# Computing part of an attention output projection transposed: 512 + 128 output columns per block instead of 320 + 320

## The chip, the cores and the metric

The kernel runs on one core of one Trainium2 chip. The metric is the device time of one execution in microseconds (us). Most executions of one kernel agree within 0.1 to 0.2%, so differences of a few tenths of a microsecond can only be read in the trace, and differences of about one need the median of several executions.

## The reference, cut to what matters

```python
x = A_x                                   # 1 x 2048 x 640, bf16
xn = _layernorm(x)
s = attention(xn) @ wo                    # 32 heads of 192; the last 512 keys of each cache; wo: 6144 x 640
g = silu(ffn(xn))                         # SwiGLU FFN, 640 -> 1536 -> 640
return x + s * g
```

The kernel handles the heads in 16 pairs, and the 2048 rows in 4 blocks of 512. For each pair and block it computes queries, scores, the product with V (PV), and adds the pair's share of `@ wo` to a sum in SBUF, the core's working memory.

## The kernel before

Every matmul of the main loop contracts 64 of the 128 partitions. `lo` is partitions 0 to 63 and `hi` is 64 to 127, and the two halves of TensorE's rows ("row groups" below) work side by side, each on a bank of its own of PSUM, the memory that matmuls write to. The output projection of one tile of 128 rows is one unit in two parts; between the parts the two row groups swap banks, which a small GpSimd memset with semaphores makes safe:

```python
    def wo_turn(st, i, qt, turn):
        ps = st["sc"]
        for j in range(3):                       # 3 chunks of 128 of the pair's 384 head columns
            for k, r in enumerate((lo, hi)):     # low, high, low, high, ...
                n = k ^ turn
                m = nc.tensor.matmul(
                    ps[:, n, 0:HD], OTs[i][r, 3 * qt + j, :], pairs[i // NB]["wo"][r, j, n * HD : (n + 1) * HD],
                    start=(turn == 0 and j == 0), stop=(turn == 1 and j == 2), skip_group_check=True,
                )
                after(m, st)
        if turn == 0:
            turned(m, st)
```

`OTs[i]` is the attention output of a block, normalised by ScalarE (`O_b`) and turned by a DMA transpose (`OT_b`), in two halves of two row tiles each. `HD` is 320. The projection of a block is issued two blocks later, woven between the PV halves of that block:

```python
    def woven(i):
        (a, b), (w, x, y, z) = (pv(i, 0), pv(i, 1)), (wo_tile(i - 2, qt) for qt in range(4))
        for part in (*a[:2], drop, w[0], *b[:2], w[1], x[0], *a[2:], x[1], y[0], *b[2:], y[1], z[0]):
            part()
        held.append(z[1])
```

In the stretch of a pair the loads of a coming pair stand behind blocks 0, 1 and 2, all on SyncE's queue:

```python
            if b == 0 and pr + 2 < NPAIR:
                load_k(pr + 2)
            elif b == 1 and pr + 2 < NPAIR:
                load_wq(pr + 2)
            elif b == 2:
                load_wo(pr + 1)
```

The softmax here doesn't subtract the row's maximum and nothing guards it: scores larger than these inputs give would overflow.

## Time and profile before

| | before |
|---|---|
| median of the first 3 runs | 922.86 us (922.59 to 923.6) |
| profiled run | 922.45 us, of which the page shows a span of 920.7 us |
| matmuls in the trace | 11086 |
| TensorE, VectorE, ScalarE busy | 99%, 63%, 52% |

The prediction below shows the head of the page, the waits and the windows. Here are the groups of the page that the change touches: line, engine, operation, output and inputs, shape, count, then busy us and mean ns of one, and idle time of the engine before them.

```profile
L440 PE MATMUL mm<-xnT,wq_p 64*128 64x512 bf16 x1890 | 240.2, 376 | 0.0
L601 DVE TENSOR_TENSOR sacc<-sacc,sc 128x640 f32<-128x640 f32 x200 | 164.2, 821 | 87.0 <-PE sc L576 87.0
L576 PE MATMUL sc<-wo_p,OT_b 64*128 64x320 bf16 x2592 | 217.3, 296 | 0.0
L479 PE MATMUL mm<-V_p,p_t 64*128 64x193 bf16 x3520 | 186.4, 242 | 0.0
```

L440 is the queries, L576 the output projection, L479 PV, L601 the add of a row tile to its sum. A matmul's record (376 ns at 512 columns) is longer than the distance to the next start on its row group (216 ns), so the records overlap and no busy share tells whether TensorE is full. The starts do.

For comparing traces I split the span into a **ledger**: opening (up to the first down-projection matmul), FFN (from there to the first 64-row query matmul), each pair (first score to the next pair's first score, called the **period** below), the last pair (first score to the last matmul) and the tail (start of the last matmul to the end). Before: 38.21, 128.88, then 41.67, 45.96, twelve times 47.03 and 47.26, last pair 49.23, tail 4.00 (the 1.09 us from the first query to the first score makes up the rest).

### The profile page before, as it was taken

Reading aid. Unit: us, or ns where it says so; the run is one execution under the profiler, and the core shown is the slowest. Engines: PE = TensorE matmul, PEld = TensorE weight load, DVE = VectorE, ACT = ScalarE, POOL = GpSimd, SP = SyncE. Lnnn points to the kernel's source line nnn. Section 1 sums busy time; section 2 is a strip of 40 time slices with the busy share of each in tenths; the row PEclk is TensorE's granted clock in tenths of the full one; section 3 lists DMA queues with packets and bytes.
Section 4 is the critical chain, followed back from the end, with each engine's and each line's share of the span. In section 5 each row is a group of like instructions: output and inputs, shape, how many; then the busy total and the mean of one; then the engine's idle time right before and its main releaser. Section 6 shows DMA issues by size and latency. Waiting matters only on the chain.

```text
span 920.7 us, 25767 instructions
## 1 busy us (share of the span) xinstructions
PE 914.6 (99%) x11086; PEld 625.9 (68%) x11102; DVE 575.8 (63%) x847; ACT 474.6 (52%) x850; POOL 101.9 (11%) x390
## 2 busy tenths in 40 slices
PE   9999999999999999999999999999999999999998
PEld 5455556575858585868686767676777777676666
DVE  6343331467676767676766667676767676767656
ACT  4222222556464646565556565655555555556461
POOL 0000000000000000000000000000000000002978
PEclk9999999999999999999999999999999999999999
DMA  9330510045644444435536262635271717163524
GB/s 308 64 75 18 110 35 1 1 78 89 92 74 85 82 83 83 79 87 70 97 62 104 60 108 53 113 48 119 44 122 36 130 37 126 31 129 86 130 62 142
DMA packets 243762, 77.18 MB, mean 84 GB/s; under 512 B 224576, under 2 KB 243648, under 8 KB 243648
## 3 DMA queue, kind: packets, MB, share of 16 engines
q1 hardware_dynamic: 243216, 75.14, 41.9%
q8 instruction: 87, 1.43, 0.7%
q10 hardware_dynamic: 432, 0.39, 0.2%
q14 instruction: 27, 0.22, 0.1%
HBM read 39.45 MB, written 2.62 MB: 46 GB/s over the span
## 4 chain that ended last, share of the span: by engine, by line
PE 98%; POOL 0%; DMA 0%; DVE 0%; issue 0%; POOLq 0%; ACT 0%; DVEq 0%
PE mm L440 22%; PE sc L576 19%; PE sc L454 18%; PE mm L479 16%; PE sc L277 11%; PE mm L299 6%; PE sc L548 2%; PE mm L531 2%; POOL ob L636 0%; PE gu L277 0%; PE mm L548 0%; PE mm L312 0%; DMA x_t<-in_A_x_dram 0%; PE sc L479 0%; PE sc L531 0%
## 5 line engine op out<-in xcount | busy, mean ns | idle before, releaser
L458 ACT ACTIVATE p_t<-sc 128x1024 bf16<-128x1024 f32 x254 | 253.0, 1023 | 128.2 <-PE sc L454 128.2
L445 DVE TENSOR_REDUCE qT<-mm 128x512 bf16<-128x1024 f32 x189 | 231.1, 1223 | 95.3 <-PE mm L440 92.8
L509 ACT ACTIVATE O_b<-mm,r 128x192 bf16<-128x192 f32 x486 | 165.0, 422 | 180.8 <-issue 156.3
L440 PE MATMUL mm<-xnT,wq_p 64*128 64x512 bf16 x1890 | 240.2, 376 | 0.0
L601 DVE TENSOR_TENSOR sacc<-sacc,sc 128x640 f32<-128x640 f32 x200 | 164.2, 821 | 87.0 <-PE sc L576 87.0
L576 PE MATMUL sc<-wo_p,OT_b 64*128 64x320 bf16 x2592 | 217.3, 296 | 0.0
L454 PE MATMUL sc<-qT,khat 64*128 64x512 bf16 x1524 | 198.2, 376 | 0.0
L479 PE MATMUL mm<-V_p,p_t 64*128 64x193 bf16 x3520 | 186.4, 242 | 0.0
L479 PEld LDWEIGHTS <-p_t 64*128 64x128 bf16 x3584 | 162.9, 93 | 12.1
L440 PEld LDWEIGHTS <-wq_p 64*128 64x128 bf16 x1890 | 105.7, 94 | 93.4 <-issue 0.5
L576 PEld LDWEIGHTS <-OT_b 64*128 64x128 bf16 x2592 | 140.4, 94 | 21.4
L454 PEld LDWEIGHTS <-khat 64*128 64x128 bf16 x1536 | 85.9, 94 | 79.8
L564 POOL MEMSET turn_t<- 128x1 f32 x328 | 32.5, 99 | 691.9 <-PE mm L479 469.7
L285 DVE TENSOR_TENSOR hT<-sc,sg 128x512 bf16<-128x512 f32 x46 | 31.7, 691 | 83.7 <-ACT sg L284 83.7
L284 ACT ACTIVATE sg<-sc 128x512 bf16<-128x512 f32 x46 | 27.3, 597 | 73.4 <-PE sc L277 71.9
L277 PE MATMUL sc<-xnT,wg_sb 128*128 128x512 bf16 (+1 forms) x248 | 59.5, 353 | 0.7
L277 PE MATMUL sc<-xnT,wu_sb 128*128 128x512 bf16 (+1 forms) x259 | 60.2, 354 | 0.1
L299 PE MATMUL mm<-wd_sb,hT 128*128 128x320 bf16 x384 | 56.6, 299 | 0.0
L498 DVE RECIPROCAL r<-mm 128x4 f32<-128x4 f32 x124 | 22.6, 182 | 46.9 <-PE mm L479 36.1
L299 PEld LDWEIGHTS <-hT 128*128 128x128 bf16 x384 | 37.6, 98 | 18.9
L277 PEld LDWEIGHTS <-wu_sb 128*128 128x128 bf16 x285 | 27.1, 98 | 26.9 <-issue 0.2
L277 PEld LDWEIGHTS <-wg_sb 128*128 128x128 bf16 x285 | 27.1, 98 | 22.7
(69 smaller groups left out, 374.9 us busy)
## 6 DMA issues: line engine op xcount, KB each, us to landing
wo_p<-in_A_wo_dram SPq DMA_DIRECT2D x16, 480.0 KB, 4.4
K_p<-in_A_k_cache_dram SPq DMA_DIRECT2D x32, 192.0 KB, 3.3
V_p<-in_A_v_cache_dram SPq DMA_DIRECT2D x32, 192.0 KB, 3.0
wq_p<-in_A_wq_dram SPq DMA_DIRECT2D x64, 80.0 KB, 3.0
wq_p<-in_A_wq_dram SPq DMA_DIRECT2D x16, 160.0 KB, 3.4
x_r<-in_A_x_dram SPq DMA_DIRECT2D x16, 160.0 KB, 4.7
x_t<-in_A_x_dram SPq DMA_DIRECT2D x14, 160.0 KB, 3.0
OT_b<-O_b SPq DMA_TRANSPOSE x124, 3.0
```

The lines of the kernel that those rows point to most:

```text
L277: nc.tensor.matmul(out, w_sb[:, c, f * P : (f + 1) * P], xnT[:, c, qc], start=(c == 0), stop=(c == NC - 1),)
L285: nc.vector.tensor_tensor(hTs[b][:, f, :], u, sg[:], ALU.mult)
L299: nc.tensor.matmul(dn[:, 0:HD], hTs[b][:, f, ti * P : (ti + 1) * P], wd_sb[:, f, cols], start=(f == 0), stop=(f == NF - 1),)
L440: nc.tensor.matmul(q_ps[:, h, :], pairs[pr]["wq"][r, c, j * P : (j + 1) * P], xnT[r, c, b * 512 : (b + 1) * 512], start=(c == 0), stop=(c ...
L445: nc.vector.reduce_sum(qTs[i][:, j, :], q_ps[:, :, :].rearrange("p h n -> p n h"), axis=AX.X)
L454: nc.tensor.matmul(sc[:, h, :], khat[r, j, ks], qT[r, j, :], start=(j == 0), stop=(j == 2))
L458: nc.scalar.activation(p_t[:, :, :], sc[:, :, :], ACT.Exp, scale=scale)
L479: m = nc.tensor.matmul(acc[:, k, h * 256 : h * 256 + Dh + 1], Ps[i][kc][r, h, qt * P : (qt + 1) * P], V_p[r, kc, h, 0 : Dh + 1], start=(p ...
L509: nc.scalar.activation(O_b[:, qt, h, :], a_k[:, h, 0:Dh], ACT.Copy, scale=r[:, k, h, :])
L564: st["turn"] = nc.gpsimd.memset(turn_t[:], 0.0)
L576: m = nc.tensor.matmul(ps[:, n, 0:HD], OTs[i][r, 3 * qt + j, :], pairs[i // NB]["wo"][r, j, n * HD : (n + 1) * HD], start=(turn == 0 and j ...
L601: nc.vector.tensor_tensor(s_t, s_t, sc[:, :, 0:HD], ALU.add)
```

## The change

The first 512 output columns of blocks 0 to 2 are computed as before, but 512 wide, two row tiles to a unit. The last 128 columns are computed transposed: the weights are stationary and the 512 rows of the block stream, which gives 128 columns x 512 rows in one unit. This makes 30 matmuls of 512 columns out of 48 of 320, thus fewer instructions for the same number of streamed columns. The sum, the gate and x for those columns are then kept transposed, and turned back by a DMA at the end. Block 3 stays as it was, so that the last tiles can end as before. Along with it, units were reordered (in all pairs, the first one having a list of its own), the weight loads moved among the scores, and the stores at the end became whole blocks, two of three on ScalarE's queue. VectorE, which normalises two half blocks of the first pair in ScalarE's place, now takes the second half of block 0 and not the first (last lines of the diff). The core of the diff, cut:

```diff
+    def wo_rest(ps, i, r=slice(0, P), first=True, end=True):
+        for j in range(3):
+            nc.tensor.matmul(
+                ps.rearrange("p (t q) -> p t q", q=P), pairs[i // NB]["wo"][r, j, MC:D],
+                OTs[i][:, :, :].rearrange("p (t j) q -> p j t q", j=3)[r, j, :, :],
+                start=(first and j == 0), stop=(end and j == 2),
+            )
 ...
+        def rest():
+            sc = sc_tile()
+            for n, r in enumerate((lo, hi)):          # low, low, low, high, high, high
+                wo_rest(sc[:, n, :], i, r)
+            for n in range(2):
+                add_sum(pr + n, s_t[:, b, :], sc[:, n, :])
+
+        if b == MB:
+            return [unit([(qt, cols) for cols in HALVES]) for qt in range(4)]
+        return [unit([(2 * h + k, MAIN) for k in range(2)]) for h in range(2)] + [[rest]]
 ...
-    def woven(i):
 ...
+    FIRST = """0a0 0b0 0a1 0b1 0e0 1b0 1a0 1b1 2b0 1a1 2b1 2w0 2x0 2w1 2a0 2x1 2a1 2y0 3a0 3y0 3a1 3x0
+        3b0 3x1 3w0 3b1 3w1"""
+    LATER = """0a0 0b0 0y0 0x0 0a1 0x1 0w0 0b1 0w1 1x0 1a0 1x1 1b0 1w0 1a1 1w1 1z0 1b1 1z1 1y0 2b0 1y1
+        2y0 2b1 2x0 2a0 2x1 3w0 2a1 3w1 2w0 3a0 2w1 3b0 3a1 3y0 3x0 3b1 3x1"""
 ...
+            if pr + 2 < NPAIR and b in (2, 3):
+                (load_k, load_wq)[b - 2](pr + 2)
+            elif pr and b == 1:
+                load_wo(pr)
 ...
-                divide(i, q2, acc, (0, 1) if q2 == i else ())
+                divide(i, q2, acc, (0, 1) if i < 2 and q2 else ())
```

In the order strings a name is block, unit, part: `a` and `b` are the two PV halves of a block (two row tiles each), `w` and `x` the two 512-column units of the block two before the one named (so `2x` belongs to block 0), `y` its transposed unit (where that is a block 3, `w x y z` are its four row tiles), `e` a query.

## The prediction

> **What bounds the kernel now.** I read the page first: its busy shares and the chain that ended last.
>
> ```profile
> span 920.7 us, 25767 instructions
> PE 914.6 (99%) x11086; PEld 625.9 (68%) x11102; DVE 575.8 (63%) x847; ACT 474.6 (52%) x850; POOL 101.9 (11%) x390
> ...
> PE 98%; POOL 0%; DMA 0%; DVE 0%; issue 0%; POOLq 0%; ACT 0%; DVEq 0%
> PE mm L440 22%; PE sc L576 19%; PE sc L454 18%; PE mm L479 16%; PE sc L277 11%; PE mm L299 6%; PE sc L548 2%; PE mm L531 2%; POOL ob L636 0%; PE gu L277 0%; PE mm L548 0%; PE mm L312 0%; DMA x_t<-in_A_x_dram 0%; PE sc L479 0%; PE sc L531 0%
> ```
>
> TensorE is on the chain for 98% of the span. A busy share of 99% alone does not prove it full, since a matmul record (376 ns) is longer than its slot, so I asked the view of waits, TensorE alone, who holds it up:
>
> ```profile
> engine line waited for: us in total, times, longest us
> PE gu L225 <- DVE zero_t L174: 1.2, 1, 1.2
> PE tp L326 <- DVE xn L262: 0.2, 1, 0.2
> ```
>
> Two waits, both in the first 6 us. Then the windows, one per pair of heads (columns: length, then each engine's busy time):
>
> ```profile
> 353.51:400.54 47.03, 47.03 (x666) 33.91 (x664) 32.62 (x45) 26.80 (x48) 2.38 (x24) 1.00 0.44 82
> 400.54:447.57 47.03, 47.03 (x666) 33.92 (x664) 32.62 (x45) 26.80 (x48) 2.38 (x24) 1.00 0.51 82
> 447.57:494.60 47.03, 47.03 (x666) 33.92 (x664) 32.61 (x45) 26.80 (x48) 2.38 (x24) 1.00 0.48 79
> ```
>
> Every pair takes exactly 47.03 us at full clock: an issue-limited loop with no jitter from a wait. Last, the timeline of TensorE in one stretch of PV and output projection (start, length, line):
>
> ```profile
> 466.17 0.85 PE L479 MATMUL mm<-V_p,p_t 64*128 64x193 bf16 x16
> 466.83 0.59 PE L576 MATMUL sc<-wo_p,OT_b 64*128 64x320 bf16 x6
> 467.24 0.85 PE L479 MATMUL mm<-V_p,p_t 64*128 64x193 bf16 x16
> 467.91 0.99 PE L576 MATMUL sc<-wo_p,OT_b 64*128 64x320 bf16 x12
> 468.72 0.85 PE L479 MATMUL mm<-V_p,p_t 64*128 64x193 bf16 x16
> ```
>
> Differences of starts give the slots. All matmuls here contract 64 rows, and a matmul on rows 0-63 ("low") and one on rows 64-127 ("high") run together. Twelve matmuls from 467.91 to 468.72 are six steps of 0.135 us; sixteen from 467.24 to 467.91 are eight of 0.083. Single records show the pairing: low at 466.835, high at 466.855, next low at 466.970, next high at 466.990. So the high one starts 20 ns after the low one. Averaged over the trace a step costs 215.9 ns at 512 columns, 135.7 at 320 and 83.4 at 193. Check: a pair of heads has 60 query and 48 score steps of 512, 128 PV steps of 193 and 96 output steps of 320: 23.31 + 10.68 + 13.03 = 47.02 us. The loop is the sum of its steps. The question is therefore how many step times the new order of matmuls needs.
>
> **What the Trainium skill says.** "TensorE: Matmul & The Clock Gate", Back-to-back issue gap: the warm gap is N/2.4 + 2.5 ns. The trace agrees: 512/2.4 + 2.5 = 215.8 against 215.9, and 135.8 against 135.7. So at equal columns only 2.5 ns per removed step is saved. Same page, The mechanism: "MATMULs are pc-monotone in start AND end — strict FIFO, no reordering", and only weight loads are pulled ahead. The trace agrees as far as it can: in the kernel before low and high strictly alternate, so no matmul there ever stands behind a busy row group that it does not need. "TensorEngine Tiling (Array Packing)", Key Properties: tiles operate independently and can execute matmuls in parallel. Here they do, 20 ns apart. It does not say that a later one may overtake.
>
> **The change, part by part.**
>
> 1. Output projection of blocks 0-2. Before: 4 row tiles x 2 halves x 3 chunks x 2 row groups = 48 matmuls of 320, 24 steps, 24 x 135.7 = 3.26 us. After: 24 matmuls of 512 (12 steps) for the first 512 columns, and 6 matmuls of 512 (3 steps) for the last 128, transposed with the weights stationary: 15 x 215.9 = 3.24. The columns streamed are the same (7680), so a block gains about 0.02 us. With 16 pairs x 3 blocks that is 48 x 0.02 = 0.9 us.
>
> 2. FFN down projection, blocks 0-2: 96 x 135.9 against 60 x 216.0 is 13.05 - 12.96 = 0.09 us a block, 0.3 in all.
>
> 3. The order of the six transposed matmuls. The code loops over the row group outside and over the chunk inside, and the listing of instructions of the built kernel keeps that: low, low, low, high, high, high. There are 41 such units in 64-row form (2 in the first pair, 3 in each of 13 others), and 164 neighbouring matmuls on the same row group, where the kernel before has none. In strict order the low ones start at 0, 216 and 432 ns. The first high one may start only behind the third low one, at 452, the others at 668 and 884; the low row group sits idle from 648, and the high one sat idle until 452. The next PV low starts at 904 and its high at 1100; the second PV low follows at 1120. In ideal alternation that second low would have been at 648 + 83 = 731. So a unit loses 1120 - 731 = 389 ns; afterwards the high group lags by 63 ns instead of 20, which costs the following steps nothing. 41 x 0.389 = 15.9 us. This lies on TensorE, beside nothing. The last two pairs use 128 rows, where order does not matter.
>
> 4. VectorE. Adds per pair: before 16 x 0.821 = 13.1 us. After: 6 of 1024 columns at about 1.22 (the query reduction over 1024 takes 1.223), 6 of 512 at about 0.69 (the FFN gate on 512 takes 0.691) and 4 x 0.821, in all 14.7. VectorE goes from 32.6 to 34.2 of 47 us: room left. Laid out by hand over a stretch with these durations, and 0.21 us from the last matmul of a unit to its add, each accumulator is free before it is next written; the tightest place (third block, first 512-column unit) has some 0.25 us to spare. Cost 0.
>
> 5. Issuing K, Wq and Wo loads among the scores: they are wanted a pair later, and no wait on them stands in the list above. Gain 0. Reordering the first pair: its stretch, 190.41 to about 208.8, is already the sum of its steps (18.2 us) within 0.2. Gain 0 to 0.1.
>
> 6. Tail. TensorE is followed by about 4 us of VectorE, GpSimd and a store, and the final tiles of block 3 are as before. Block stores on ScalarE's queue end well before them, and the 128-column transposes back happen some 10 us earlier. About 0.
>
> Sum: 922.9 - 0.9 - 0.3 + 15.9 = **937.6 us**.
>
> **Rivals.** (a) The row groups take matmuls from queues of their own, so three high ones start beside three low ones. For it: tiles are called independent, and nothing in this trace shows a blocked head. The author, who alternates everywhere else, gave each row group its own bank here, as if they ran together. Against: the in-order statement. Time: 922.9 - 1.2 = 921.7. (b) One matmul can be parked per row group, so the high one waits one slot fewer: 41 x (0.389 - 0.216) = 7.1 us, time 928.8. (c) VectorE becomes the bound inside a stretch, as a 1024-column add holds two banks for 1.2 us and the transposed unit needs two adds one after the other. A missed 0.25 us in each of 13 stretches is 3 us on top of any of the others; 63% busy and no wait before speak against it. (d) The tail gets longer, because a whole block's store waits for its transposed part: 1 to 2 us. The final store comes from block 3, so I doubt it.
>
> **Range and chances.** I give strict order about 6 in 10, rival (a) 3 and (b) 1. A range for 8 in 10 must reach from (a) to strict order plus a little of (c): 921.0 to 939.5, with 937.6 as the likeliest. Both ends are within 2% of 922.86 (904.4 to 941.3): faster 0.01, same 0.94, slower 0.05.
>
> **What the profile after would show.** Right in step 1: TensorE's output steps of 512 spaced 216 ns. Right in step 3: periods of about 48.1 us instead of 47.03 (3 x 0.389 less 0.06), the same in each pair from the second on, and within the transposed units starts 216 ns apart for six matmuls in a row instead of 20 and 196 by turns, with no wait named. Rival (a): periods of 46.97. Rival (c): waits of TensorE for VectorE's adds. The prediction is wrong if the high matmuls of that unit start within 20 ns of the low ones.

## The result, and the profile after

| | before | after |
|---|---|---|
| median | 922.81 us (922.59 to 923.86, 6 runs) | 923.25 us (923.0 to 923.64, 6 runs) |
| profiled run | 922.45 us, span 920.7 | 923.57 us, span 921.8 |
| matmuls in the trace | 11086 | 10193 |

The ratio after to before is 1.0003, with a 95% interval of 0.999 to 1.0016. Ratios here are computed as the mean time of one kernel's fast runs over that of the other's of the same rounds, so they are not quite the ratio of the medians that I quote. The forecast of 937.6 us was wrong: no loss of 15 us came. The time is about where it was.

The head of the page after, and its chain:

```profile
span 921.8 us, 23762 instructions
PE 914.7 (99%) x10193; PEld 527.3 (57%) x10193; DVE 594.6 (65%) x844; ACT 473.7 (51%) x841; POOL 91.0 (10%) x302
...
PE 98%; DMA 1%; DVE 0%; SPq 0%; POOLq 0%; POOL 0%; issue 0%; DVEq 0%
```

Two thousand instructions fewer, weight loads (PEld) from 68% down to 57%, and TensorE still on the chain for 98%. The view of waits of the kernel after, TensorE alone, has one new line:

```profile
PE sc L619 <- DMA OT_b<-O_b: 1.2, 1, 1.2
```

A 512-column unit waits once, for a transposed attention output. The windows of two pairs after (length, then each engine's busy time with its number of records, TensorE clock, DMA share, GB/s):

```profile
258.65:305.62 46.97, 46.97 (x614) 27.91 (x611) 33.97 (x46) 26.84 (x49) 1.78 (x18) 1.00 0.42 81
305.62:352.58 46.96, 46.96 (x613) 27.91 (x611) 33.96 (x46) 26.83 (x49) 1.78 (x18) 1.00 0.38 82
```

The period is 46.96 us, the figure of rival (a) and not the 48.1 of strict order. The timeline of TensorE around one transposed unit after (start, length, line):

```profile
244.72 0.57 PE L619 MATMUL sc<-wo_p,OT_b 64*128 64x320 bf16 x6
245.13 0.81 PE L587 MATMUL sc<-OT_b,wo_p 64*128 64x512 bf16 x6
245.78 0.83 PE L499 MATMUL mm<-V_p,p_t 64*128 64x193 bf16 x16
```

L587 is the transposed unit. From its start to that of the PV half behind it are 0.65 us, three steps of 0.216 us: the six matmuls run in three pairs. The single records show it: starts at 245.131 and 245.134, 245.347 and 245.350, 245.563 and 245.566. The program has them as low, low, low, high, high, high, and still a high one starts 3 ns after each low one. (The 3 ns are not the point: that distance is 3 to 26 ns from one trace to another, at the same period of 46.96 us.) So the first high one overtook two low ones that were still waiting.

VectorE's adds after, by group:

```profile
L632 DVE TENSOR_TENSOR s_m<-s_m,sc 128x1024 f32<-128x1024 f32 x82 | 100.2, 1222 | 49.3 <-PE sc L619 43.0
L632 DVE TENSOR_TENSOR s_t<-s_t,sc 128x512 f32<-128x512 f32 x82 | 56.2, 686 | 18.3 <-PE sc L587 16.8
```

They cost what was reckoned (1.22 and 0.69 us), and TensorE waits for none of them.

The ledger says where the time went. Each row is read off the two traces of the table above:

| part | before | after | difference |
|---|---|---|---|
| FFN | 128.88 | 128.61 | -0.27 |
| first pair | 41.67 | 42.97 | +1.29 |
| second pair | 45.96 | 45.88 | -0.08 |
| pairs 3 to 14, each | 47.03 | 46.96 | -0.07, in all -0.81 |
| pair 15 | 47.26 | 47.17 | -0.09 |
| last pair | 49.23 | 49.14 | -0.09 |
| tail | 4.00 | 4.56 | +0.56 |
| sum without the opening | 882.45 | 882.97 | +0.52 |

The sum, +0.5 us, answers to the medians (923.25 - 922.81 = 0.44). The opening was left out: it was 38.21 before and 38.81 in this profile, but 38.1 to 38.9 in the traces of the changed kernel and its variants below and 38.2 to 39.4 in those of the kernel before. Two things are left to explain beside the failed step: 1.3 us lost in the first pair and 0.56 us in the tail.

The loss in the first pair is that one wait. The timeline of TensorE there, after:

```profile
198.49 0.81 PE L619 MATMUL sc<-wo_p,OT_b 64*128 64x512 bf16 x6
200.55 1.47 PE L619 MATMUL sc<-wo_p,OT_b 64*128 64x512 bf16 x12 [1.25 <-DMA OT_b<-O_b]
```

Unit `2w0` starts at 198.49 and `2x0` would follow at 199.14. It starts at 200.55, because it reads row tiles 2 and 3 of block 0, the second half of the transposed output. That DMA was issued at 195.89 and landed at 200.51, 4.6 us later; the median of all 124 transposes is 2.7. A packet of instruction fetch was under way meanwhile (197.88 to 198.80), and the last section counts how often the two go together. Before, the same transpose was just as late (issued 195.81, landed 200.35), but the kernel took row tiles 0 and 1 first and came to tile 2 only at 201.62:

```profile
201.62 0.99 PE L576 MATMUL sc<-wo_p,OT_b 64*128 64x320 bf16 x12
```

So the delay was there all along, hidden by the old order.

### The profile page after: what moved, and what is told of

It is laid out like the page before. It is cut to its first block, busy times and chain, and to the rows that moved or that the text cites. A ratio compares the mean times of both kernels' runs of the same rounds, so it can differ in the third digit from the quotient of the medians.

```text
span 921.8 us, 23762 instructions
## 1 busy us (share of the span) xinstructions
PE 914.7 (99%) x10193; PEld 527.3 (57%) x10193; DVE 594.6 (65%) x844; ACT 473.7 (51%) x841; POOL 91.0 (10%) x302
## 4 chain that ended last, share of the span: by engine, by line
PE 98%; DMA 1%; DVE 0%; SPq 0%; POOLq 0%; POOL 0%; issue 0%; DVEq 0%
PE mm L460 22%; PE sc L474 18%; PE sc L619 16%; PE mm L499 16%; PE sc L282 11%; PE mm L321 6%; PE sc L587 3%; PE sc L579 2%; PE mm L551 2%; PE mm L579 1%; DMA x_t<-in_A_x_dram 1%; DMA OT_b<-O_b 1%; PE gu L282 0%; PE mm L330 0%; PE sc L551 0%; PE sc L499 0%
## 5 line engine op out<-in xcount | busy, mean ns | idle before, releaser
L619 PE MATMUL sc<-wo_p,OT_b 64*128 64x512 bf16 (+1 forms) x1608 | 179.2, 345 | 1.2 <-DMA OT_b<-O_b 1.2
L499 PE MATMUL mm<-V_p,p_t 64*128 64x193 bf16 x3520 | 178.3, 242 | 0.0
L460 PEld LDWEIGHTS <-wq_p 64*128 64x128 bf16 x1890 | 91.8, 94 | 112.0 <-issue 0.7
L632 DVE TENSOR_TENSOR s_m<-s_m,sc 128x1024 f32<-128x1024 f32 x82 | 100.2, 1222 | 49.3 <-PE sc L619 43.0
L474 PEld LDWEIGHTS <-khat 64*128 64x128 bf16 x1536 | 74.8, 94 | 91.0
L619 PEld LDWEIGHTS <-OT_b 64*128 64x128 bf16 x1608 | 75.6, 94 | 46.2 <-DMA OT_b<-O_b 1.7
L605 POOL MEMSET turn_t<- 128x1 f32 x246 | 24.4, 99 | 699.1 <-PE mm L499 494.2
L632 DVE TENSOR_TENSOR s_t<-s_t,sc 128x512 f32<-128x512 f32 x82 | 56.2, 686 | 18.3 <-PE sc L587 16.8
L632 DVE TENSOR_TENSOR s_o<-s_o,sc 128x640 f32<-128x640 f32 x52 | 42.7, 821 | 15.9 <-PE sc L619 14.8
L321 PE MATMUL mm<-wd_sb,hT 128*128 128x512 bf16 (+1 forms) x240 | 46.7, 347 | 0.0
```

What stands on the lines that cost most here:

```text
L321: nc.tensor.matmul(dn, at, by, start=(f == 0), stop=(f == NF - 1))
L460: nc.tensor.matmul(q_ps[:, h, :], pairs[pr]["wq"][r, c, j * P : (j + 1) * P], xnT[r, c, b * 512 : (b + 1) * 512], start=(c == 0), stop=(c ...
L474: nc.tensor.matmul(sc[:, h, :], khat[r, j, ks], qT[r, j, :], start=(j == 0), stop=(j == 2))
L499: m = nc.tensor.matmul(acc[:, k, h * 256 : h * 256 + Dh + 1], Ps[i][kc][r, h, qt * P : (qt + 1) * P], V_p[r, kc, h, 0 : Dh + 1], start=(p ...
L619: m = nc.tensor.matmul(ps[:, k, 0 : cols.stop - cols.start], OTs[i][r, 3 * qt + j, :], pairs[i // NB]["wo"][r, j, cols], start=(turn == 0 ...
L632: nc.vector.tensor_tensor(to, to, ps, ALU.add)
```

## The experiments

Twelve runs were made, all correct. The theories after the result: **A**, a matmul of one row group may overtake waiting ones of the other, but only a few of them; **B**, it may overtake any number (queues of their own); and for the first pair and the tail, the parts of the change one by one.

### The changed kernel once more

No edit.

> The changed kernel unaltered, a second profile, to see how much of its ledger repeats. In the first pair of profiles the changed kernel lost 0.60 us before its first down projection, won 0.27 in the FFN, lost 1.26 in the first pair of heads, won 0.88 in pairs 1 to 13, 0.16 in the last two pairs and lost 0.55 after the last matmul. If the 0.60 and the 0.55 belong to single executions and not to the change, they move here by some tenths; if they belong to the change, both stand. The wait of 1.25 us of TensorE for the transposed attention output in the first pair should stand if it is set by the order of the units.

Measured: 923.27 us (4 runs) against 922.79 (7 runs of before), ratio 1.0004, 0.9989 to 1.0019. The trace has the same ledger (first pair 42.96, periods 46.96, tail 4.56), with an opening of 38.29. So the first pair and the tail belong to the program and the opening does not.

### Low and high alternating in the transposed unit

```diff
-            for n, r in enumerate((lo, hi)):
-                wo_rest(sc[:, n, :], i, r)
+            for j in range(3):
+                for n, r in enumerate((lo, hi)):
+                    nc.tensor.matmul(..., start=(j == 0), stop=(j == 2))
```

> The six 64-row matmuls of the 128-column unit alternate low, high, low, high, low, high. Strict order (the prediction's step 3): the changed kernel loses 0.389 us in each of 41 units, so this one is 15.9 us faster than it, near 907. Row groups that take matmuls independently (rival a): the unit already takes 0.65 us in the trace, so nothing changes: 923.2 within 0.5, period of a pair 46.97.

Measured: 922.99 us, ratio 1.0002 (0.9987 to 1.0017); periods 46.96, as without the edit. The order that I charged with 15.9 us costs nothing at all: with three matmuls in a run there is nothing to win back.

### How far the overtaking goes

In the kernel before, whose order alternates throughout, some pairs got longer runs of one row group in the source, each with its own length (I count pairs from 1, the text on record from 0): output parts and scores in runs of 3 (pairs 3 and 9), PV in 4 (pair 11), queries in 5 (pair 5), PV in 8 (pair 7), two query units together in 10 (pair 13), and PV of one block of the first pair in 16.

```diff
-            for kc in range(KC):
-                for n, r in enumerate((lo, hi)):
+            order = [(p, kc, n) for kc in range(KC) for n in range(2)]
+            if runs:
+                order = [(q, kc, n) for n in range(2) for q in (p, p + 1) for kc in range(KC)]
```

> The kernel before, with low and high matmuls grouped in runs instead of alternating, a different length in different pairs of heads, odd pairs untouched as controls (47.03 us). Pair 2: output projection 3 and 3; pair 4: queries 5 and 5; pair 6: PV 8 and 8; pair 8: scores 3 and 3; pair 10: PV 4 and 4; pair 12: queries 10 and 10 once a block; pair 0, second block: PV 16 and 16. Strict order adds (run length - 1) steps less 43 ns per group: pair 2 +7.3, pair 4 +9.9, pair 6 +8.7, pair 8 +6.2, pair 10 +6.6, pair 12 +7.6 us, the 16s +2.4 us in pair 0. Independent row groups: all periods 47.0 within 0.1. A limited look-ahead: the short runs free, the long ones not, and the length where it starts tells its depth.

Measured: 932.42 us, one run. The run of 16 in the first pair is easiest to see, since its two accumulators have different names. Timeline of TensorE in this run (`mm` and `sc` are the two accumulators; the low row group starts on both in turn, then the high one):

```profile
195.34 0.83 PE L479 MATMUL mm<-V_p,p_t 64*128 64x193 bf16 x8
196.01 0.57 PE L479 MATMUL sc<-V_p,p_t 64*128 64x193 bf16 x5
196.35 0.25 PE L479 MATMUL mm<-V_p,p_t 64*128 64x193 bf16 x1
196.42 0.24 PE L479 MATMUL sc<-V_p,p_t 64*128 64x193 bf16 x1
```

Eight and five low ones run alone, 83 ns apart; the first high one (back on `mm`) starts at 196.347, 8 ns after the 13th low one. Three low ones were then still waiting. In the runs of 10 queries the first high one starts at 752.376, 8 ns after the 7th low one (752.368): again three waiting. The windows of the pairs with runs of 4 (first line), 5 and 8:

```profile
636.75:683.78 47.03, 47.03 (x667) 38.11 (x665) 32.62 (x46) 26.77 (x48) 2.35 (x24) 1.00 0.49 81
352.87:400.32 47.45, 47.45 (x668) 37.13 (x666) 32.67 (x46) 26.76 (x48) 2.35 (x24) 1.00 0.45 81
447.35:495.50 48.15, 48.15 (x666) 38.98 (x664) 32.47 (x46) 26.77 (x48) 2.35 (x24) 1.00 0.44 79
```

The pairs left alone stay at 47.03, but for two that share the cost of their neighbour's runs of 8 and 10. Against that, runs of 3 (both pairs) and 4 cost 0.00, runs of 5 cost 0.42, runs of 8 cost 1.28 (48.16 and the next period's 47.18 together), runs of 10 cost 5.13 (49.06 and 50.13 together, 0.3 of it a wait named in the view, for a swap of banks) and the runs of 16 cost 1.8 (43.49 against 41.67). Theory A with a reach of three gives, for a run of n by itself, n - 4 steps in which only one row group works. For 10 that is 4 runs x 6 x 0.216 = 5.2 us, and for 16, 2 x 12 x 0.0834 = 2.0 us: close to what was measured. For 5 and 8 the same product (12 x 1 x 0.216 = 2.6, 16 x 4 x 0.0834 = 5.3) is far too much. For 5 the trace shows why. Only once, in the first run, does low work alone, for two steps (starts at 351.380 and 351.595; a part of an output unit stands in that run, so the count by n doesn't hold for it). From then on low stays two steps ahead: at 354.593 its first score starts, before the last two high queries at 354.631 and 354.847. So the later runs lose nothing more, and two steps of 0.216 are the whole 0.42; the runs of 5 therefore say little about the reach. That it is the same with the runs of 8 is likely, but not shown. B is refuted: with queues of any depth no run would have cost anything. So is strict order, which charges already the runs of 3 and 4. Whether the reach of three is one window over all waiting matmuls or a short queue for each row group, these runs can't tell.

### The first pair: unit x later

```diff
-    FIRST = """... 2b1 2w0 2x0 2w1 2a0 2x1 2a1 2y0 3a0 3y0 3a1 3x0 3b0 3x1 3w0 3b1 3w1"""
+    FIRST = """... 2b1 2w0 2a0 2w1 2x0 2a1 2x1 2y0 3a0 3b0 3y0 3a1 3x0 3b1 3w0 3x1 3w1"""
```

> Only the order of units in the first pair is changed: the second 512-column unit of block 0 comes 1.3 us later, behind PV work. Theory: its wait of 1.25 us for the second half of the transposed output of block 0 (landed at 200.5 us in the trace) goes, so 1.2 us less, about 922.0, and TensorE's wait for the DMA falls under 0.2 us. Rival: another wait takes its place (an accumulator or a turn of the row groups) and the time stays within 0.3 us of 923.2.

Measured: 922.45 us, ratio 0.9995 (0.9979 to 1.0012). The first pair went from 42.97 to 42.05 us, and the wait for the DMA is gone from the view of waits. In its place stands another:

```profile
PE mm L499 <- ACT O_b L529: 0.3, 1, 0.3
```

PV half `2a0` now comes too early: its accumulator is still being read by ScalarE's division of block 1. The gap costs 0.51 us, and the second pair 0.25 (46.13 instead of 45.88).

### The first pair: row tiles of block 1 pulled forward

```diff
-    FIRST = """0a0 0b0 0a1 0b1 0e0 1b0 1a0 1b1 2b0 1a1 2b1 ..."""
+    FIRST = """0a0 0b0 0a1 1a0 0b1 1a1 0e0 1b0 2b0 1b1 2b1 ..."""    # the rest as in the run before
```

> The changed kernel with another order in the first pair: block 1's first half moved before the early query unit, so that each half's accumulator is free when it is next written and the second half of block 0 is used only after about 200.1 us. The run with the later unit still lost 0.51 us to an accumulator held by ScalarE. Theory: that loss goes too, the first pair falls from 42.05 to about 41.6 us, the time to about 921.9. Rival: the stall moves to a later unit and the first pair stays above 42.

Measured: 922.47 us, ratio 0.9996 (0.9981 to 1.0011), first pair 42.10. The stall moved: a PV half now starts at 196.44 instead of about 195.89, again for an accumulator that ScalarE holds (0.4 us in the view of waits). This order only exchanges one early request for another.

### The first pair: both kept apart

The first two orders tell what is needed: unit `2x0` later than in the change, and `2a0` no earlier than there.

```diff
-    FIRST = """0a0 0b0 0a1 0b1 0e0 1b0 1a0 1b1 2b0 1a1 2b1 2w0 2x0 2w1 2a0 2x1 2a1 2y0 ..."""
+    FIRST = """0a0 0b0 0a1 0b1 0e0 1b0 1a0 1b1 1a1 2b0 2w0 2b1 2w1 2a0 2x0 2a1 2x1 2y0 ..."""
```

> The changed kernel with another order in the first pair only: 1a1 2b0 2w0 2b1 2w1 2a0 2x0 2a1 2x1 2y0, so that the first unit that needs the second half of block 0's transposed output begins about 1.3 us later, and PV half 2a0 begins 2.6 us after 1a1 instead of the 1.3 us of first_late. Expected, if the wait for that transpose and the hold of the accumulator are all that the first pair loses: no wait for the DMA and none for ScalarE, at most 0.15 us for the add of unit x; first pair 41.7 to 41.9 us instead of 42.97, second pair 45.88, time about 922.0. Rival: the stall moves again (the first half of the transposed output, needed 0.67 us earlier, is late): first pair at 42.1 or more, time 922.4 or more.

> The kernel of first_spread once more, in five rounds, to see whether its gain over the kernel before is real. From the ledger of its first trace (first pair 41.73, periods 46.96, tail 4.56, opening 38.1 to 38.8) I expect 921.7 to 922.3 us, about 0.8 us under the kernel before (ratio 0.9991), with a first pair of 41.7 to 41.9 and no wait of TensorE after the first 6 us. If the gain of the first look was chance, it lies at 922.6 or above.

Measured: 921.92 us (921.61 to 922.15, 4 runs) against 922.66 (922.36 to 923.26, 7 runs), ratio 0.999 (0.9975 to 1.0005), and in a second call 922.11 (921.75 to 922.65, 5 runs) against 922.81 (922.5 to 923.88, 9 runs), ratio 0.9992 (0.9978 to 1.0005). The first pair took 41.73 us in both traces, and no wait of TensorE is left in the pairs. The transpose was late here too (issued 195.59, landed 199.90), but `2x0` starts only at 200.17, behind the second part of `2w` and a PV half:

```profile
198.86 0.81 PE L619 MATMUL sc<-wo_p,OT_b 64*128 64x512 bf16 x6
200.17 0.81 PE L619 MATMUL sc<-wo_p,OT_b 64*128 64x512 bf16 x6
```

The two intervals both reach just over 1, so the gain of 0.7 us isn't settled by them. But of the nine times eight lie at or under 922.15, and all sixteen of the kernel before at or over 922.36; and the ledger agrees with the gain: the span without the opening is 881.75 us in both traces, 0.70 under the 882.45 of before (882.70 in the second trace of before). The second call lists one more wait in the opening (0.9 us for the layer norm), which the same code did not have in the other. Of the versions run, this is the fastest.

### The new columns in the old order, everything else undone

The columns stay; the units of all pairs stand in my transcription of the old weave, loads, stores and the division of the first blocks as before (the list of the first pair, `FIRST`, is left out here).

```diff
-    LATER = """0a0 0b0 0y0 0x0 0a1 0x1 0w0 0b1 0w1 1x0 1a0 ..."""
+    LATER = """0a0 0w0 0b0 0w1 0x0 0a1 0x1 0y0 0b1 1a0 1w0 1b0 1w1 ..."""
```

> The 512 + 128 columns alone: units in the order of the kernel before, K, Wq and Wo loads back in the stretches of PV and output projection, all block stores on SyncE's queue. If the columns carry the gain: period of a pair 46.96 and FFN part 128.61 us as in the changed kernel. If the reordering caused the loss in the first pair, the loss is gone there (first pair 41.6 to 41.7 us from first score to first score, as before with 41.67); if the loss comes from the columns themselves, because a unit now needs two row tiles of the transposed output, TensorE still waits there, 0.5 to 1.3 us.

Measured: 986.71 us against 922.6, ratio 1.0694 (1.0676 to 1.0712). The period is 51.76 us, 4.8 over the change. TensorE's waits in this run:

```profile
PE mm L499 <- ACT O_b L529: 42.8, 27, 1.7
PE mm L460 <- ACT O_b L529: 14.3, 14, 1.1
```

PV and queries wait for accumulators that ScalarE is still dividing. The last PV half of one block (`0b1`) and the first of the next (`1a0`) stand side by side here, because a block has only five parts of output work to put between instead of eight. The FFN part is 128.61 us, as expected. The first pair takes 43.59 us, with 0.2 us of waiting for the transposed output and 1.5 for an accumulator, so this run can't tell whether the old order alone would have kept its 41.67.

### Only the order undone, with y between the blocks

The run before undoes several things at once, and its order is unkind. So this one is the changed kernel with the old weave from the second pair on, and `y` behind `b1`.

```diff
+    LATER = """0a0 0w0 0b0 0w1 0x0 0a1 0x1 0b1 0y0 1a0 1w0 1b0 1w1 1x0 1a1 1x1 1y0 1b1 1y1 1z0
+        2a0 1z1 2w0 2b0 2w1 2x0 2a1 2x1 2b1 2y0 3a0 3w0 3b0 3w1 3x0 3a1 3x1 3b1 3y0"""
```

> The changed kernel with one thing undone: from the second pair on the units stand in the old weave (first half of PV of two tiles, then output units between, as before), with the transposed unit y put between the last PV half of one block and the first of the next, where the run columns_alone had nothing. Loads, block stores and the first pair are those of the changed kernel. Theory 'the new columns need the new order': the accumulators are still held by ScalarE's divisions, only less long, as 0.65 us of y now stands in each of the four gaps; from the gaps of 2.0, 1.9 and 1.4 us there, I expect about 2 to 3 us per pair over 46.96, a period of 49 to 50 us and a time of about 955 to 965. Rival 'the loss of columns_alone came from my transcription, or from the loads': a period of 46.96 to 47.2, and a time of 923 to 926.

Measured: 934.83 us (4 runs) against 922.66, ratio 1.0133 (1.0116 to 1.015); period 47.88 us. My expectation of 49 to 50 was too high, and the rival's 46.96 to 47.2 was too low. The waits in this run:

```profile
PE mm L499 <- ACT O_b L529: 7.0, 25, 0.4
```

So most of the 7% of the run before was due to that transcription (the loads don't change the period, as the next run shows), but not all: with one unit between, the accumulator still comes up to 0.4 us late at about two places per pair (25 waits). The view names 7.0 us of the 13 x 0.92 = 12 us that the pairs lose; I did not assign the rest. So the new columns need another order than these two; the change's own is worth 12 us against this weave.

### Loads back in the stretch

```diff
+            if name == "0b1":
+                load_k(pr + 2)
+            elif name == "1b1":
+                load_wq(pr + 2)
+            elif name == "2b1":
+                load_wo(pr + 1)
```

(and the lines that load among the scores removed)

> K, Wq and Wo loads issued in the stretches again, as before. Prediction's step 5: nothing moves: periods 46.96, first pair as in the changed kernel (42.96), time 923.2 within 0.5. Rival: the loads delay the transposes of the attention output and TensorE waits in every pair.

Measured: 924.7 us, one run. The periods stay at 46.96, but the first pair takes 44.66 instead of 42.97:

```profile
PE sc L587 <- DMA OT_b<-O_b: 1.6, 1, 1.6
PE sc L619 <- DMA OT_b<-O_b: 1.2, 1, 1.2
```

A second wait for a transposed output appears. With the loads in the stretch, the transpose of the second half of block 1 stands behind the five issues of Wq on SyncE's queue: issued 203.10, landed 206.26, for a unit that would have started at about 204.6 and starts at 206.40. In this one execution, moving the loads is worth 1.7 us in the first pair and nothing in the period of the others.

### Block stores back on SyncE's queue

```diff
-            store_block(b, nc.scalar if b else nc.sync)
+            store_block(b, nc.sync)
 ...
-            store_block(2, nc.scalar)
+            store_block(2, nc.sync)
```

> Block stores of blocks 1 and 2 back on SyncE's queue. After the last matmul the changed kernel takes 4.56 us in every profile, the kernel before 4.00 to 4.04; the last store lands 3.11 after the last matmul in both, so the difference lies behind the last landing. If the stores on ScalarE's queue cause it, this falls to about 4.0. If it is the closing sequence of the program itself, it stays at 4.5.

Measured: 925.54 us, one run; tail 6.24 us instead of 4.56. SyncE's timeline near the end (start and length of issues of its DMA queue):

```profile
911.64 1.80 SPq L738 DMA_TRANSPOSE x_b<-o_t  x1
917.08 0.38 SPq L757 DMA_DIRECT2D out_dram<-x_b  x1
917.55 2.27 SPq L764 DMA_DIRECT2D out_dram<-x_b  x3
919.91 0.52 SPq L752 DMA_DIRECT2D out_dram<-x_b  x1
```

L738 turns the last transposed part back, L757 is the store of block 2, which must wait for it, and everything behind it on this queue waits too. Here the transpose took 5.4 us to land (917.03), and the last store is issued at 919.91. In columns_alone, which has the stores on the same queue, it landed in 3.7 us and the tail is 4.49. In both, the store of block 1 was issued on the same queue 0.48 us ahead of it; in the nine other traces with the change, where that store is on ScalarE's queue, the transpose landed in 2.4 us. So the stores on SyncE's queue cost between nothing and 1.7 us, by how late that transpose lands; on ScalarE's queue the wait is off the path. With one trace of each, how late it can land stays open. The question of the expectation has a plain answer: from the last landing to the end this run takes 1.45 us and the changed kernel 1.44, so the stores on ScalarE's queue are not what makes the tail longer.

### The kernel before once more

No edit.

> The kernel before, profiled a second time, for the parts of the span that can vary between executions. Theory 'the tail is the program's, the opening is chance': tail 4.00 to 4.04 us again, opening anywhere from 38.1 to 39.4, periods 47.03. If the tail is 4.5 here, the 0.55 us of the changed kernel's tail is chance and not the change.

Measured: 922.8 us, one run; opening 38.31, periods 47.03, first pair 41.92, tail 4.02. So two executions of the kernel before differ by 0.25 us in the first pair (here an output unit starts at 203.85, just after the transpose of block 1's first half has landed at 203.81), and the 1.29 us lost there by the change are good to about that. The tail of 4.0 belongs to the kernel before (4.00, 4.02, and 4.04 in the run with longer runs), that of 4.4 to 4.6 to all kernels with the change but stores_on_sync. Of the 0.56 us, nothing lies ahead of the last store's landing: it comes 3.11 us after the start of the last matmul in both traces (919.767 - 916.664 = 3.10 before, 920.335 - 917.222 = 3.11 after). The rest is what the engines do after it, semaphores and drains: 0.90 us before and 1.44 after. Most of it has a place in the traces: from GpSimd's clearing of its semaphores to its next semaphore event are 0.21 us in the two traces of the kernel before and in the run with longer runs, and 0.52 to 0.66 in all eleven with the change (0.65 in the one after). Why GpSimd takes longer there stays open; no run took it apart.

## Why the prediction was right or wrong

**Step 3 failed, the order of the six transposed matmuls.** It said that "In strict order the low ones start at 0, 216 and 432 ns. The first high one may start only behind the third low one, at 452", and charged 41 x 0.389 = 15.9 us. The runs show in its place: the high one starts 3 ns after the first low one, the unit takes three steps (0.65 us), and alternating the source changes nothing (periods 46.96 both ways). That is the prediction's own sign of being wrong. What the runs fit is a look-ahead: a matmul whose row group is free passes up to three waiting matmuls of the other row group. In a run of three it has to pass two, in one of four three, and both cost nothing. The kernel before couldn't show this, as every matmul in its main loop alternates; its perfect alternation fits strict order and look-ahead alike, and the in-order statement that the prediction quotes from the skill, which this trace did not test, decided for the first. I gave rival (a) 3 in 10, and its time of 921.7 leaves out only the 1.3 and 0.56 us below. Its mechanism was only half right: there is a limit, which this change does not meet. Rival (b), one parked matmul, is refuted by the same numbers.

**Steps 1 and 2 were right.** A pair gains 0.07 us (0.06 predicted) and the FFN 0.27 (0.3 predicted). The intended gain comes to 1.3 us in all (0.27 + 0.81, and 0.08, 0.09 and 0.09 in the other pairs).

**Step 4 was right.** VectorE's busy time per pair is 33.97 us (34.2 predicted, from 32.62), and rival (c), a wait for its adds, did not come. But step 4 looked at VectorE only, and the danger in the stretch was ScalarE: the two runs with the old weave lose 0.9 and 4.8 us per pair, with waits for accumulators that it still divides. The change avoids this by its order, which step 5 dealt with only as the first pair's.

**Step 5 was mis-sized.** "Gain 0" for the loads is right from the second pair on, but in the first it was 1.7 us (one run). "Gain 0 to 0.1" for the reordering of the first pair was +1.3 us of loss, for the order there asks for the second half of block 0's transposed output 2.5 us sooner (199.14 instead of about 201.6), before it has landed. I had counted the steps of the old stretch, not the landing times that the new order would meet. The run with both kept apart gives the 1.3 us back.

**Step 6 was off by half a microsecond.** "About 0" was 0.56. Rival (d), the block's store waiting for its transposed part, showed only with the stores on SyncE's queue (1.7 us in one run, none in another).

So the gain went like this: 1.3 us came, 1.3 were lost again at one wait in the first pair, and 0.56 behind the last store.

## What to carry to other kernels

When neighbouring matmuls use different rows of the array, their order in the program matters only beyond a short look-ahead (here, with two groups of 64 rows, three waiting ones), so let measured runs of different length decide before paying for an order or fearing it. A wider unit needs its whole input at its first part: check the landing times of the transfers that the new order meets first, not only the sum of the matmuls. And where a change removes units that stood between two uses of an accumulator, look at who still reads the accumulator; here the same arithmetic cost between 0 and 7% depending almost only on the order.

## What the Trainium skill lacked or had wrong

- "TensorE: Matmul & The Clock Gate", The mechanism: "MATMULs are pc-monotone in start AND end — strict FIFO, no reordering" does not hold between 64-row tiles on different partitions. A high matmul starts 3 ns after the first of three low ones that precede it in the program (245.131 and 245.134), thus ahead of two of them.
- "TensorEngine Tiling (Array Packing)", Key Properties, says that tiles operate independently, and gives no limit. The runs show one: the first high matmul started 8 ns after the 13th of 16 low ones and after the 7th of 10, so with three still waiting (and the next low one 9 ns after the 7th of those 10 high ones, 753.690 against 753.681); runs of 3 and 4 cost 0.00 us, longer ones up to 5.13 us in two pairs.
- "DMA: Bandwidth & Descriptors", DMA Transpose (X-bar), lists constraints and alternatives, but not how long one transpose takes to land, and no page says what delays it. Here the median was 2.7 us. The transpose of the second half of block 0 in the first pair took 4.2 to 4.7 us in twelve of the fourteen traces, each with a 16 KB packet of instruction fetch inside its flight; in the two in which no packet ran before its last 0.16 us it took 2.8. In the trace after, 61 of the 124 transposes shared time with such a packet (16 or 8 KB), and 15 of them took over 4 us. Of the other 63 (median 2.7) a single one took over 3: 4.1 us, behind a block store on its queue. That the packets are the cause is likely from this, but no edit tested it.
